# A two-layer kernel on one core: 512 instead of 288 columns a matmul in the second product, the last 64 columns of two blocks as a pair of column tiles

## Chip, cores, metric

The kernel runs on one core of one Trainium2 chip. The metric is the device time of one execution in microseconds; lower is better. The granted TensorE clock is the share of its full speed that the profiler recorded.

## The reference

```python
B, S, D, F = 1, 2048, 576, 4608          # all bf16
def reference(x, w1, b1, w2, b2):
    h = einsum("bsd,df->bsf", x, w1) + b1      # first product, 576 -> 4608
    r = where(h > 0, h, 0)
    h = r * r
    return einsum("bsf,fd->bsd", h, w2) + b2   # second product, 4608 -> 576
```

The output has 576 columns, which is 512 + 64. The widest matmul of these kernels writes 512 columns of float32, which fills one of the program's tiles in PSUM, the memory that matmuls write to.

## The kernel before

The 2048 rows go through in four blocks of 512 (`SB`). For each block the first product makes the hidden tile `hT`, transposed: 36 pieces of 128 hidden columns by 512 rows. The second product takes 128 rows of it at a time as weights (a "row block", 16 in all) and streams `w2` past them, 576 output columns in two halves of 288 (`DH`), 36 steps each.

```python
    DH = D // 2                                   # 288
    # ... weights and x are loaded; x is transposed into xT ...

    def a_rows(sb, ...):                          # most of the first product: pairs of 64-row tiles
        for j in range(NJ):
            # ...
            for i in range(NC):
                keep(nc.tensor.matmul(bx[:], lhsT=w1_h[0:H, LO_C[i], jc], rhs=xT[0:H, LO_W[i], :], ...))
                keep(nc.tensor.matmul(by[:], lhsT=w1_h[H:P, UP_C[i], jc], rhs=xT[H:P, UP_W[i], :], ...))
            evac_h(...)                           # ScalarE: relu + bias; VectorE: square, into hT

    def a_full(sb, order):                        # four pieces: full-array matmuls of 512 columns
        # ... and two pairs of 64-row tiles, `pair`; then evac_h

    def phase_b(sb, hT, last=False, dups=()):     # second product
        for jj in range(RT):                      # 4 row blocks
            # ...
            po = [ps_o.tile([P, 512], FP32, name="po", tag="po") for _ in range(2)]
            o_sb = opool.tile([P, D], BF16, name="o_sb", tag="o_sb")

            def mmb(i, ft, h):
                keep(nc.tensor.matmul(
                    po[h][:, 0:DH],
                    lhsT=hT[:, ft, jj * P:(jj + 1) * P],
                    rhs=w2_sb[:, ft, h * DH:(h + 1) * DH],
                    start=(i == 0), stop=(i == NFT - 1)))

            def evac(h):                          # VectorE: + b2, to bf16
                keep(nc.vector.tensor_tensor(out=o_sb[:, h * DH:(h + 1) * DH], in0=po[h][:, 0:DH],
                                             in1=b2_bc[:, h * DH:(h + 1) * DH], op=ALU.add))

            if last and jj == RT - 1:             # very last row block: one half after the other
                for h in range(2):
                    for i, ft in enumerate(ft_order):
                        mmb(i, ft, h)
                    evac(h)
                    keep(nc.sync.dma_start(out=out2[...], in_=o_sb[:, h * DH:(h + 1) * DH]))
                continue
            for i, ft in enumerate(ft_order):
                for h in range(2):
                    mmb(i, ft, h)
            for h in range(2):
                evac(h)
            keep(nc.sync.dma_start(out=out2[rt * P:(rt + 1) * P, :], in_=o_sb[:]))

    # order of the stages
    a_full(0, "k_outer"); a_rows(0, ...); a_rows(1); a_full(1, "rows_first")
    phase_b(0, ...); phase_b(1, ...)
    a_full(2, "g_outer"); a_rows(2); a_rows(3); a_full(3, "rows_first")
    phase_b(2, ...); phase_b(3, ..., last=True)
```

Of the kernel before, what the change touches and what calls it, by code (L numbers as in the profile page):

```python
# [9 lines left out]
ACT = mybir.ActivationFunctionType  # L10
ALU = mybir.AluOpType
BF16 = mybir.dt.bfloat16
FP32 = mybir.dt.float32
# [4 lines left out]
def kernel(  # L18
# [9 lines left out]
    nc = tc.nc  # L28
    keep = tc.keep_in_program_order
    P = 128  # L30
    H = 64
    x2 = x.flatten_outer_dims()
    out2 = out.flatten_outer_dims()
    S, D = x2.shape
    F = w1.shape[1]
    NFT = F // P
    NC = D // H
    NK = NC // 2
    G = 4
# [3 lines left out]
    assert D == 576 and S % 512 == 0 and F % (2 * P) == 0  # L43
    SB = 512
    RT = SB // P
    DH = D // 2

    const = ctx.enter_context(tc.tile_pool(name="const", bufs=1))
    wpool = ctx.enter_context(tc.tile_pool(name="wpool", bufs=1))
# [1 line left out]
    hpool = ctx.enter_context(tc.tile_pool(name="hpool", bufs=2))  # L51
    rpool = ctx.enter_context(tc.tile_pool(name="rpool", bufs=4))
    opool = ctx.enter_context(tc.tile_pool(name="opool", bufs=3))
    ps_h = ctx.enter_context(tc.tile_pool(name="ps_h", bufs=4, space=PSUM))
    ps_o = ctx.enter_context(tc.tile_pool(name="ps_o", bufs=4, space=PSUM))

# [18 lines left out]
    def load_w1n8(eng, h):  # L75
        src = w1[NK * P:D, 0:GW].rearrange("p (i h f) -> p i h f", h=2, f=P)
        keep(eng.dma_start(out=w1n8[h * H:(h + 1) * H, :, :], in_=src[:, :, h, :]))
# [16 lines left out]
    nc.gpsimd.dma_start(out=b1_rows[0:NFT, :], in_=b1.rearrange("(ft p) -> ft p", p=P))  # L94
    load_w1n8(nc.gpsimd, 0)
    load_w1n8(nc.gpsimd, 1)
    warm = const.tile([P, 1], FP32, name="warm")
    keep(nc.scalar.activation(out=warm[:], in_=nc.const_aps.tensor(0.0, [P, 1], FP32), func=ACT.Relu))  # L98

# [11 lines left out]
    def dup_windows(sb):  # L111
        xT = xT_blk[sb]
        keep(nc.vector.tensor_copy(out=xT[0:H, SPC:SPC + 4, :], in_=xT[H:P, E3:E3 + 4, :]))  # L113
        keep(nc.vector.tensor_copy(out=xT[H:P, SPC:SPC + 4, :], in_=xT[0:H, O:O + 4, :]))  # L114
# [8 lines left out]
    w2_sb = wpool.tile([P, NFT, D], BF16, name="w2_sb")  # L123
# [6 lines left out]
    b2_bc = const.tile([P, D], BF16, name="b2_bc")  # L130
# [18 lines left out]
    def make_b1T():  # L149
        b1T_ps = ps_o.tile([P, P], BF16, name="b1T_ps", tag="po")  # L150
        keep(nc.tensor.transpose(b1T_ps[:], b1_rows[:], ident[:]))  # L151
        keep(nc.vector.tensor_copy(out=b1T[:], in_=b1T_ps[:, 0:NFT]))

    hTs = {}
# [4 lines left out]
    def evac_h(sb, bank, ft):  # L159
        r = rpool.tile([P, SB], BF16, name="r", tag="r")  # L160
        keep(nc.scalar.activation(out=r[:], in_=bank[:], func=ACT.Relu, bias=b1T[:, ft:ft + 1], scale=1.0))  # L161
        keep(nc.vector.tensor_tensor(out=hTs[sb][:, ft, :], in0=r[:], in1=r[:], op=ALU.mult))  # L162

    def a_rows(sb, dup_at=None, dup_sb=None):
        xT = xT_blk[sb]
        for j in range(NJ):
            if j == dup_at:
                dup_windows(dup_sb)
            bx = ps_h.tile([P, SB], FP32, name="ph", tag="ph")
            by = ps_h.tile([P, SB], FP32, name="ph", tag="ph")  # L170
            jc = slice(j * P, (j + 1) * P)
            for i in range(NC):
                keep(nc.tensor.matmul(bx[:], lhsT=w1_h[0:H, LO_C[i], jc], rhs=xT[0:H, LO_W[i], :],  # L173
                                 start=(i == 0), stop=(i == NC - 1)))
                keep(nc.tensor.matmul(by[:], lhsT=w1_h[H:P, UP_C[i], jc], rhs=xT[H:P, UP_W[i], :],  # L175
                                 start=(i == 0), stop=(i == NC - 1)))
            evac_h(sb, bx, G + j)
            evac_h(sb, by, G + NJ + j)

    def a_full(sb, order):  # L180
        xT = xT_blk[sb]
        banks = []
        for g in range(G):
            pool, tag = (ps_o, "po") if g < 2 else (ps_h, "ph")
            banks.append(pool.tile([P, SB], FP32, name="pn", tag=tag))

        def pair(i, start, stop):
            keep(nc.tensor.matmul(banks[2 * i][:], lhsT=w1n8[0:H, i, :], rhs=xT[0:H, SPC, :],  # L188
                             start=start, stop=stop))
            keep(nc.tensor.matmul(banks[2 * i + 1][:], lhsT=w1n8[H:P, i, :], rhs=xT[H:P, E3, :],  # L190
                             start=start, stop=stop))

        def full(g, k, start, stop):
            keep(nc.tensor.matmul(banks[g][:], lhsT=w1n[:, k, g * P:(g + 1) * P], rhs=xT[:, O + k, :],  # L194
                             start=start, stop=stop))

        if order == "rows_first":
            for i in (1, 0):
                pair(i, True, False)
            for g in (2, 3, 0, 1):  # L200
                for k in range(NK):
                    full(g, k, False, k == NK - 1)
                evac_h(sb, banks[g], g)
        else:
            if order == "k_outer":
                for k in range(NK):
                    for g in range(G):
                        full(g, k, k == 0, False)
                    if k == 1:
                        make_b1T()  # L210
            else:
                for g in (2, 3, 0, 1):
                    for k in range(NK):
                        full(g, k, k == 0, False)
            for i in (1, 0):
                pair(i, False, True)
                evac_h(sb, banks[2 * i], 2 * i)
                evac_h(sb, banks[2 * i + 1], 2 * i + 1)

    ft_order = list(range(G))  # L220
    for j in range(NJ):
        ft_order += [G + j, G + NJ + j]

    def phase_b(sb, hT, last=False, dups=()):
        for jj in range(RT):
            if jj < len(dups):
                dup_windows(dups[jj])
            rt = sb * RT + jj
            po = [ps_o.tile([P, 512], FP32, name="po", tag="po") for _ in range(2)]
            o_sb = opool.tile([P, D], BF16, name="o_sb", tag="o_sb")  # L230

            def mmb(i, ft, h):
                keep(nc.tensor.matmul(  # L233
                    po[h][:, 0:DH],
                    lhsT=hT[:, ft, jj * P:(jj + 1) * P],
                    rhs=w2_sb[:, ft, h * DH:(h + 1) * DH],
                    start=(i == 0),
                    stop=(i == NFT - 1),
                ))

            def evac(h):
                keep(nc.vector.tensor_tensor(  # L242
                    out=o_sb[:, h * DH:(h + 1) * DH],
                    in0=po[h][:, 0:DH],
                    in1=b2_bc[:, h * DH:(h + 1) * DH],
                    op=ALU.add,
                ))

            if last and jj == RT - 1:
                for h in range(2):  # L250
                    for i, ft in enumerate(ft_order):
                        mmb(i, ft, h)
                    evac(h)
                    keep(nc.sync.dma_start(out=out2[rt * P:(rt + 1) * P, h * DH:(h + 1) * DH], in_=o_sb[:, h * DH:(h + 1) * DH]))
                continue
            for i, ft in enumerate(ft_order):
                for h in range(2):
                    mmb(i, ft, h)
            for h in range(2):
                evac(h)  # L260
            keep(nc.sync.dma_start(out=out2[rt * P:(rt + 1) * P, :], in_=o_sb[:]))

    for (j0, j1) in [(0, 1), (1, 2), (2, 4), (4, 6), (6, 8), (8, 10), (10, 12)]:
        load_w1(nc.sync, 0, j0, j1)
# [14 lines left out]
    load_xT(3)  # L279
    a_rows(1)  # L280
    a_full(1, "rows_first")
    phase_b(0, hTs[0], dups=(2, 3))
    phase_b(1, hTs[1])
    alloc_hT(2)
    a_full(2, "g_outer")
    a_rows(2)
    alloc_hT(3)
    a_rows(3)
    a_full(3, "rows_first")
    phase_b(2, hTs[2])  # L290
    phase_b(3, hTs[3], last=True)

# [29 lines left out]
```

## Time and profile before

| | before |
|---|---|
| time, median of the first 3 runs | 292.98 us (292.62 to 293.26) |
| profiled execution: time, span | 292.11 us, 290.3 us |
| PE busy | 285.7 us, 98% |
| second product | 1152 matmuls of 288 columns, 141.4 us busy, in two stretches |

These lines are from the page of the kernel before (PE is TensorE's matmuls, PEld its weight loads, DVE VectorE, ACT ScalarE, POOL GpSimd; L233 is line 233 of the kernel): the busy time of each engine, the shares of the chain of waits (the chain that ended last, by engine and by line), and groups of instructions. In a group the columns are busy time, mean ns of one, and idle time of the engine before them. A group's busy time counts overlapping instructions once, so busy time divided by count is the pace, while the mean of one is its length from start to end.

```profile
PE 285.7 (98%) x2409; PEld 178.0 (61%) x2412; DVE 81.5 (28%) x189; ACT 94.2 (32%) x154; POOL 2.7 (1%) x10
...
PE 98%; ACT 0%; issue 0%; DVE 0%
PE po L233 49%; PE ph L173 42%; PE pn L194 5%; PE wps L61 1%; PE ph L175 1%; PE pn L188 1%; PE ta L138 0%; ACT xTw L143 0%; DVE o_sb L242 0%; ACT xTw L144 0%; PE tb L141 0%; PE tb L142 0%; PE b1T_ps L151 0%; PE pn L190 0%
...
L233 PE MATMUL po<-w_sb,hT 128*128 128x288 bf16 x1152 | 141.4, 286 | 0.0
L233 PEld LDWEIGHTS <-hT 128*128 128x128 bf16 x1152 | 112.7, 98 | 28.8
...
L194 PE MATMUL pn<-xTw,w1n 128*128 128x512 bf16 x61 | 14.0, 379 | 0.8 <-ACT xTw L143 0.4
L194 PEld LDWEIGHTS <-w1n 128*128 128x128 bf16 x64 | 6.0, 98 | 8.0 <-issue 1.4
...
L242 DVE TENSOR_TENSOR o_sb<-po,b_bc 128x288 bf16<-128x288 f32 x32 | 13.3, 453 | 123.9 <-PE po L233 123.9
```

PE is busy for 98% of the span, and 98% of the chain is PE: no other engine is what the end waits for, apart from the start, the last addition and its store. The 1152 matmuls of line 233 took 141.4 us, 122.7 ns apiece, though each lasts 286 ns: they are pipelined. Their weight loads last 98 ns each and hide behind them.

The chain in order of time (start, length, what) shows the two stretches of the second product and the last addition.

```profile
72.67 3.40 PE pn L194 x15
76.07 70.56 PE po L233 x576
...
216.77 70.58 PE po L233 x576
287.37 0.46 DVE o_sb L242
```

A stretch of 576 matmuls takes 70.56 us, which is 122.5 ns each. This is the timeline where row tiles (64 x 128) give way to full-array matmuls (128 x 128):

```profile
71.91 0.38 PE L188 MATMUL pn<-xTw,w1n_89 64*128 64x512 bf16 x1
71.92 0.38 PE L190 MATMUL pn<-xTw,w1n_89 64*128 64x512 bf16 x1
72.13 0.38 PE L188 MATMUL pn<-xTw,w1n_89 64*128 64x512 bf16 x1
72.13 0.38 PE L190 MATMUL pn<-xTw,w1n_89 64*128 64x512 bf16 x1
72.67 0.59 PE L194 MATMUL pn<-xTw,w1n 128*128 128x512 bf16 x2 [0.16 <-issue]
```

Row tiles come in pairs, 0.01 us apart or less, and a pair follows the last after 0.22 us. The first full matmul starts 0.54 us after the last pair.

### The profile page before, as it was taken

The numbers are of one execution on the slowest core, as the hardware profiler recorded it, in microseconds if no ns is written. First come the engines' busy times: TensorE is split into PE (matmuls) and PEld (weight loads), VectorE is DVE, ScalarE is ACT, GpSimd is POOL, SyncE is SP. The second block draws the span as 40 slices with busy tenths as digits, with TensorE's granted clock in tenths as the row PEclk, the third lists the DMA queues.
The fourth block names the chain that finished last, engine by engine and source line by source line (L and its number), as shares of the span: only waits on it lengthen the run. The fifth ranks groups of instructions, "written<-read, shape, count | busy, mean of one in ns | idle before, by whom it ended". The sixth has DMA issues, their size and how long they took to land.

```text
span 290.3 us, 5455 instructions
## 1 busy us (share of the span) xinstructions
PE 285.7 (98%) x2409; PEld 178.0 (61%) x2412; DVE 81.5 (28%) x189; ACT 94.2 (32%) x154; POOL 2.7 (1%) x10
## 2 busy tenths in 40 slices
PE   8999999999999999999999999999999999999995
PEld 4444444444677777777744444444447777777774
DVE  3344544444531011110025444444440111100111
ACT  4566666666400000000027666666670000000000
POOL 3000000000000000000000000000000000000000
PEclk9999999999999999999999999999999999999999
DMA  7999999900000000000000000000000000000000
GB/s 203 214 212 177 255 357 265 164 1 2 0 23 0 23 20 20 23 3 20 20 23 0 3 0 2 0 2 0 2 0 2 20 24 20 21 2 23 20 20 24
DMA packets 27096, 16.05 MB, mean 55 GB/s; under 512 B 11028, under 2 KB 27040, under 8 KB 27072
## 3 DMA queue, kind: packets, MB, share of 16 engines
q1 hardware_dynamic: 26688, 15.32, 23.9%
q8 instruction: 19, 0.31, 0.4%
q10 hardware_dynamic: 288, 0.30, 0.3%
q0 software_dynamic: 96, 0.07, 0.1%
q14 instruction: 5, 0.04, 0.0%
HBM read 11.36 MB, written 2.36 MB: 47 GB/s over the span
## 4 chain that ended last, share of the span: by engine, by line
PE 98%; ACT 0%; issue 0%; DVE 0%
PE po L233 49%; PE ph L173 42%; PE pn L194 5%; PE wps L61 1%; PE ph L175 1%; PE pn L188 1%; PE ta L138 0%; ACT xTw L143 0%; DVE o_sb L242 0%; ACT xTw L144 0%; PE tb L141 0%; PE tb L142 0%; PE b1T_ps L151 0%; PE pn L190 0%
## 5 line engine op out<-in xcount | busy, mean ns | idle before, releaser
L233 PE MATMUL po<-w_sb,hT 128*128 128x288 bf16 x1152 | 141.4, 286 | 0.0
L233 PEld LDWEIGHTS <-hT 128*128 128x128 bf16 x1152 | 112.7, 98 | 28.8
L173 PE MATMUL ph<-xTw,w_h 64*128 64x512 bf16 x576 | 124.6, 376 | 0.0
L175 PE MATMUL ph<-xTw,w_h 64*128 64x512 bf16 x576 | 124.6, 376 | 0.0
L173 PEld LDWEIGHTS <-w_h 64*128 64x128 bf16 x576 | 54.1, 94 | 68.3
L161 ACT ACTIVATE r<-ph,b1T 128x512 bf16<-128x512 f32 x128 | 81.1, 685 | 41.6 <-PE ph L175 41.6
L162 DVE TENSOR_TENSOR hT<-r 128x512 bf16<-128x512 bf16 x144 | 61.2, 426 | 77.3 <-ACT r L161 76.7
L175 PEld LDWEIGHTS <-w_h 64*128 64x128 bf16 x576 | 54.1, 94 | 0.0
L242 DVE TENSOR_TENSOR o_sb<-po,b_bc 128x288 bf16<-128x288 f32 x32 | 13.3, 453 | 123.9 <-PE po L233 123.9
L161 ACT ACTIVATE r<-pn,b1T 128x512 bf16<-128x512 f32 x16 | 10.3, 688 | 78.8 <-PE pn L190 77.5
L194 PE MATMUL pn<-xTw,w1n 128*128 128x512 bf16 x61 | 14.0, 379 | 0.8 <-ACT xTw L143 0.4
L194 PEld LDWEIGHTS <-w1n 128*128 128x128 bf16 x64 | 6.0, 98 | 8.0 <-issue 1.4
L61 PE MATMUL wps<-const-bfloat16-1.0 128*128 128x512 bf16 (+1 forms) x7 | 2.9, 594 | 0.8 <-PEq L306 0.8
L113 DVE COPY xTw<-xTw 64x2048 bf16<-64x2048 bf16 x4 | 2.8, 690 | 0.4 <-ACT xTw L144 0.3
L114 DVE COPY xTw<-xTw 64x2048 bf16<-64x2048 bf16 x4 | 2.7, 687 | 0.1
L139 DVE COPY xTw<-ta 128x384 bf16<-128x384 bf16 x4 | 1.3, 358 | 4.2 <-PE ta L138 4.2
L188 PE MATMUL pn<-xTw,w1n_89 64*128 64x512 bf16 x8 | 2.4, 379 | 0.0
L190 PE MATMUL pn<-xTw,w1n_89 64*128 64x512 bf16 x8 | 2.4, 379 | 0.0
L61 PEld LDWEIGHTS <-const-bfloat16-1.0 128*128 128x128 bf16 x7 | 0.9, 135 | 2.1 <-issue 2.1
L98 ACT ACT_TABLE_LOAD x1 | 1.3, 1283 | 1.7 <-PEq L306 1.7
L138 PE MATMUL ta<-ident,x_sb 128*128 128x128 bf16 x12 | 1.6, 265 | 0.0
L143 ACT COPY xTw<-tb 128x128 bf16<-128x128 bf16 x4 | 1.1, 282 | 1.2 <-PE tb L142 1.1
(21 smaller groups left out, 10.2 us busy)
## 6 DMA issues: line engine op xcount, KB each, us to landing
w_sb<-in_w_dram SPq DMA_DIRECT2D x6, 864.0 KB, 11.4
w_h<-in_w_dram SPq DMA_DIRECT2D x14, 288.0 KB, 7.4
out_dram<-o_sb SPq DMA_DIRECT2D x15, 144.0 KB, 1.8
w_h<-in_w_dram SPq DMA_DIRECT2D x4, 144.0 KB, 4.1
w1n<-in_w_dram SPq DMA_DIRECT2D x4, 128.0 KB, 4.0
x_sb<-in_x_dram ACTq DMA_DIRECT2D x2, 144.0 KB, 3.0
x_sb<-in_x_dram SPq DMA_DIRECT2D x2, 144.0 KB, 2.8
b_bc<-in_b_dram SPq DMA_DIRECT2D x1, 144.0 KB, 7.6
```

The costliest lines, as they stand in the source:

```text
L61: keep(nc.tensor.matmul(wps[:, 0:n], lhsT=ones[:, 0:P], rhs=ones[:, 0:n], start=True, stop=True))
L113: keep(nc.vector.tensor_copy(out=xT[0:H, SPC:SPC + 4, :], in_=xT[H:P, E3:E3 + 4, :]))
L114: keep(nc.vector.tensor_copy(out=xT[H:P, SPC:SPC + 4, :], in_=xT[0:H, O:O + 4, :]))
L161: keep(nc.scalar.activation(out=r[:], in_=bank[:], func=ACT.Relu, bias=b1T[:, ft:ft + 1], scale=1.0))
L162: keep(nc.vector.tensor_tensor(out=hTs[sb][:, ft, :], in0=r[:], in1=r[:], op=ALU.mult))
L173: keep(nc.tensor.matmul(bx[:], lhsT=w1_h[0:H, LO_C[i], jc], rhs=xT[0:H, LO_W[i], :], start=(i == 0), stop=(i == NC - 1)))
L175: keep(nc.tensor.matmul(by[:], lhsT=w1_h[H:P, UP_C[i], jc], rhs=xT[H:P, UP_W[i], :], start=(i == 0), stop=(i == NC - 1)))
L188: keep(nc.tensor.matmul(banks[2 * i][:], lhsT=w1n8[0:H, i, :], rhs=xT[0:H, SPC, :], start=start, stop=stop))
L190: keep(nc.tensor.matmul(banks[2 * i + 1][:], lhsT=w1n8[H:P, i, :], rhs=xT[H:P, E3, :], start=start, stop=stop))
L194: keep(nc.tensor.matmul(banks[g][:], lhsT=w1n[:, k, g * P:(g + 1) * P], rhs=xT[:, O + k, :], start=start, stop=stop))
L233: keep(nc.tensor.matmul(po[h][:, 0:DH], lhsT=hT[:, ft, jj * P:(jj + 1) * P], rhs=w2_sb[:, ft, h * DH:(h + 1) * DH], start=(i == 0), stop=( ...
L242: keep(nc.vector.tensor_tensor(out=o_sb[:, h * DH:(h + 1) * DH], in0=po[h][:, 0:DH], in1=b2_bc[:, h * DH:(h + 1) * DH], op=ALU.add,))
```

## The change

The intent is fewer instructions for the same columns. Each row block now streams 512 columns in one matmul instead of 2 x 288. The last 64 columns are computed with the roles exchanged: the 64 columns of `w2` are the weights, and the hidden tile, 512 rows of it, streams past. Weights of 64 columns fill half of the array's columns, so two blocks are put side by side as column tiles (128 x 64), writing to partitions 0 to 63 and 64 to 127 of one PSUM tile (`phase_t`, once for each pair of blocks). The result is transposed, so a DMA turns it before it is stored. The very last row block is cut in pieces of 224, 160 and 128 columns, so that the last addition and store are small. The diff, shortened:

```diff
-    DH = D // 2
+    DM = 512
+    DT = D - DM
@@
+    b2_col = const.tile([P, 1], BF16, name="b2_col")
+    for h in range(2):
+        nc.gpsimd.dma_start(out=b2_col[h * DT:(h + 1) * DT, :], in_=b2[DM:D].rearrange("(d o) -> d o", o=1))
+    b2T = const.tile([P, 1], FP32, name="b2T")
+    nc.gpsimd.tensor_copy(out=b2T[:], in_=b2_col[:])
@@
+    t_order = ft_order[G:] + ft_order[:G]
+    EDGES = [0, 224, 384, 512]
+
+    def phase_t(sb):
+        pt = ps_o.tile([P, SB], FP32, name="pt", tag="po")
+        for i, ft in enumerate(t_order):
+            for h in range(2):
+                keep(nc.tensor.matmul(pt[h * DT:(h + 1) * DT, :], lhsT=w2_sb[:, ft, DM:D], rhs=hTs[sb + h][:, ft, :],
+                                      start=(i == 0), stop=(i == NFT - 1)))
+        oT = tpool.tile([P, SB], BF16, name="oT", tag="oT")
+        keep(nc.scalar.activation(out=oT[:], in_=pt[:], func=ACT.Identity, bias=b2T[:], scale=1.0))
+        ot = tpool.tile([P, RT, P], BF16, name="ot", tag="ot")
+        keep(nc.sync.dma_start_transpose(out=ot[:, :, :], in_=oT[:, :]))
+        for h in range(2):
+            r0 = (sb + h) * SB
+            dst = out2[r0:r0 + SB, DM:D].rearrange("(j p) d -> p j d", p=P)
+            keep(nc.sync.dma_start(out=dst, in_=ot[:, :, h * DT:(h + 1) * DT]))
@@ phase_b: the two halves, their additions and the staged last block are removed (cut here); in their place
+            o_sb = opool.tile([P, DM], BF16, name="o_sb", tag="o_sb")
+            edges = EDGES if last and jj == RT - 1 else [0, DM]
+            for d0, d1 in zip(edges, edges[1:]):
+                po = ps_o.tile([P, 512], FP32, name="po", tag="po")
+                for i, ft in enumerate(ft_order):
+                    keep(nc.tensor.matmul(po[:, 0:d1 - d0], lhsT=hT[:, ft, jj * P:(jj + 1) * P],
+                                          rhs=w2_sb[:, ft, d0:d1], start=(i == 0), stop=(i == NFT - 1)))
+                keep(nc.vector.tensor_tensor(out=o_sb[:, d0:d1], in0=po[:, 0:d1 - d0], in1=b2_bc[:, d0:d1], op=ALU.add))
+                keep(nc.sync.dma_start(out=out2[rt * P:(rt + 1) * P, d0:d1], in_=o_sb[:, d0:d1]))
@@ order of the stages
     a_full(1, "rows_first")
+    phase_t(0)
     phase_b(0, hTs[0], dups=(2, 3))
@@
     a_full(3, "rows_first")
+    phase_t(2)
     phase_b(2, hTs[2])
```

More of the change, by code (lines that the diff above doesn't have):

```diff
@@ L53 @@
     opool = ctx.enter_context(tc.tile_pool(name="opool", bufs=3))
+    tpool = ctx.enter_context(tc.tile_pool(name="tpool", bufs=2))
     ps_h = ctx.enter_context(tc.tile_pool(name="ps_h", bufs=4, space=PSUM))
@@ L228, in phase_b @@
             rt = sb * RT + jj
-            po = [ps_o.tile([P, 512], FP32, name="po", tag="po") for _ in range(2)]
-            o_sb = opool.tile([P, D], BF16, name="o_sb", tag="o_sb")
-            def mmb(i, ft, h):
-                keep(nc.tensor.matmul(
-                    po[h][:, 0:DH],
-                    lhsT=hT[:, ft, jj * P:(jj + 1) * P],
-                    rhs=w2_sb[:, ft, h * DH:(h + 1) * DH],
-                    start=(i == 0),
-                    stop=(i == NFT - 1),
-                ))
-            def evac(h):
-                keep(nc.vector.tensor_tensor(
-                    out=o_sb[:, h * DH:(h + 1) * DH],
-                    in0=po[h][:, 0:DH],
-                    in1=b2_bc[:, h * DH:(h + 1) * DH],
-                    op=ALU.add,
-                ))
-            if last and jj == RT - 1:
-                for h in range(2):
-                    for i, ft in enumerate(ft_order):
-                        mmb(i, ft, h)
-                    evac(h)
-                    keep(nc.sync.dma_start(out=out2[rt * P:(rt + 1) * P, h * DH:(h + 1) * DH], in_=o_sb[:, h * DH:(h + 1) * DH]))
-                continue
-            for i, ft in enumerate(ft_order):
-                for h in range(2):
-                    mmb(i, ft, h)
-            for h in range(2):
-                evac(h)
-            keep(nc.sync.dma_start(out=out2[rt * P:(rt + 1) * P, :], in_=o_sb[:]))
+            o_sb = opool.tile([P, DM], BF16, name="o_sb", tag="o_sb")
[7 more added lines that the diff above has]
+                keep(nc.sync.dma_start(out=out2[rt * P:(rt + 1) * P, d0:d1], in_=o_sb[:, d0:d1]))
     for (j0, j1) in [(0, 1), (1, 2), (2, 4), (4, 6), (6, 8), (8, 10), (10, 12)]:
```

## The prediction

> **What bounds it now.** TensorE. The page gives PE 98% busy, the chain of waits is 98% PE, and in the list of waits matmuls waited 1.5 us in all, before 6 us. The granted clock is 1.000. So only TensorE's stream, or the tail behind it, can count. The second product is 49% of the chain: two stretches of 70.56 us, 576 matmuls of 288 columns each, 122.5 ns a matmul.
>
> **Fixed cost of a matmul.** The Trainium skill, "TensorE: Matmul & The Clock Gate", Part 1, states N/2.4 + about 2.5 ns. This trace agrees: 122.5 ns for 288 columns; 512-column full matmuls start about every 216 ns, and so do pairs of 64-row tiles, whose two start within 10 ns.
>
> **What the change does on TensorE.** Columns streamed do not fall, if column tiles run two at a time: per row block 2 x 288 = 512 + 64, and the 64 return as 72 pairs of 512 columns. Only instruction overhead goes.
> - Removed: 1152 x 122.5 ns = 141.1 us.
> - Added: 16 row blocks x 36 x 215.8 ns = 124.3 us, and 72 pairs x 215.8 ns = 15.5 us. Net -1.3 us.
> - The last block is cut in 224, 160 and 128 columns: 72 more instructions, +0.2 us. A weight load lasts 98 ns, longer than a 128-column matmul streams, but loads overlap: the warm 128-column transposes near 4.8 us start 55 ns apart, each with its own load. I expect no load limit.
> - Four new changes of tiling. The skill, "TensorEngine Tiling (Array Packing)", Key Properties, says that a mode change drains the engine; here full to row tiles (149.70 to 150.01 us) costs 0.1 us extra, row tiles to full (72.13 to 72.67 us) 0.3 us. Estimate +0.8 us.
> - Tail: the last addition is 128 instead of 288 columns (0.46 us now) and its store smaller: about -0.3 us.
>
> Sum about -0.6 us, all on the critical path.
>
> **Off the path.** Additions of 512 columns (estimate 0.7 us) against 7.8 us of matmuls per block; one activation of about 0.7 us per pair of blocks on an idle ScalarE; the transposing DMA (those of x land in 5.6 us) and stores of 128-byte rows, behind 60 us of matmuls. The new stage reads the second block's hidden tile just after its last pieces are computed, but takes those four last, some 7 us later, while their evacuation ends 1.1 us after the matmuls; waits go by region in this trace (matmuls at 5.71 us read a tile that VectorE is still filling). I expect no new wait of TensorE.
>
> **Predicted time.** 292.4 us; 80% range 290.8 to 296.0. Faster by over 2%: 0.01; within 2%: 0.84; slower by over 2%: 0.15.
>
> **What would show it.** Pairs of the new stage start together, every 216 ns; the stage takes 15.5 us, twice; row blocks 7.77 us each; small gaps at the stage's ends; PE still 98%; the last block about 8 us.
>
> **What would make it wrong.** Mainly column tiles that do not overlap. No trace here shows a column tile; row tiles feed each half of the rows once, column tiles stream two operands through all 128. One after the other, the stage doubles: +15.5 us, about 308 us, 5% slower. The tiling page also says that column tiling disables fast weight load: if the 64-column loads show, each 25 ns in a pair costs 1.8 us. If 128-column pieces were limited by loads at 98 ns, the last block would cost 2.5 us more. A wait of TensorE at the new stage's start would cost about 1 us each.

One sentence of it is worded wrongly: "the stage takes 15.5 us, twice". The 72 pairs of its own sum are those of both stages together, so 15.5 us is the total and each stage was due at 7.8 us. The predicted time uses the total.

## More of the kernel before

One line carries a warning: line 194 has 61 matmuls and 64 weight loads. The program issues one load for each matmul, so three matmul records are missing from this trace.

## The result

The changed kernel took 291.44 us (median of 4 runs, 291.28 to 291.98) against 292.80 us (4 runs). The ratio was 0.9954, 95% interval 0.9936 to 0.9973. A ratio is the mean time of one kernel's fast runs over that of the other's of the same rounds, so it is not quite the ratio of the medians. With five rounds of unchanged copies (told below) the ratio was 0.9975, interval 0.9957 to 0.9992. The change is a gain, and a small one: well within 2%.

The page of the changed kernel, the same parts:

```profile
PE 285.7 (99%) x2052; PEld 134.1 (46%) x2052; DVE 79.7 (28%) x175; ACT 95.7 (33%) x156; POOL 4.2 (1%) x13
...
PE 98%; ACT 0%; DVE 0%; issue 0%
PE po L259 43%; PE ph L180 42%; PE pt L238 5%; PE pn L201 5%; PE wps L63 1%; PE ph L182 1%; PE pn L195 1%; PE ta L145 0%; ACT xTw L150 0%; ACT xTw L151 0%; DVE o_sb L261 0%; PE tb L149 0%; PE tb L148 0%; PE b1T_ps L158 0%; PE pn L197 0%
...
L259 PE MATMUL po<-w_sb,hT 128*128 128x512 bf16 (+3 forms) x648 | 124.8, 355 | 0.0
...
L259 PEld LDWEIGHTS <-hT 128*128 128x128 bf16 x648 | 60.7, 98 | 64.3 <-issue 0.8
...
L261 DVE TENSOR_TENSOR o_sb<-po,b_bc 128x512 bf16<-128x512 f32 (+3 forms) x18 | 11.4, 633 | 125.0 <-PE po L259 125.0
...
L238 PE MATMUL pt<-hT,w_sb 128*64 128x512 bf16 x144 | 15.9, 380 | 0.0
...
L238 PEld LDWEIGHTS <-w_sb 128*64 128x64 bf16 x144 | 8.0, 110 | 7.8 <-issue 0.8
...
L201 PE MATMUL pn<-xTw,w1n 128*128 128x512 bf16 x64 | 14.5, 379 | 0.4 <-ACT xTw L150 0.4
```

PE still fills the span. Line 238 is the new stage: 144 matmuls, each 380 ns long, in 15.9 us. That is 110 ns apiece for 512 columns, which is only possible two at a time. Its weight loads became longer (110 ns, against 94 for a row tile's and 98 for a full one), and they hide too. The busy time of weight loads in the second product fell from 112.7 to 68.7 us (60.7 + 8.0), and the kernel did not become faster by anything like that: these loads were hidden behind matmuls before and after.

The chain in order of time, and the groups of line 259 with the widths kept apart:

```profile
72.75 3.56 PE pn L201 x16
76.31 7.89 PE pt L238 x72
84.21 62.27 PE po L259 x288
...
216.62 7.89 PE pt L238 x72
224.50 62.46 PE po L259 x360
286.99 0.29 DVE o_sb L261
```

```profile
L259 PE MATMUL po<-w_sb,hT 128*128 128x512 bf16 x540 | 116.9, 379 | 0.0
...
L259 PE MATMUL po<-w_sb,hT 128*128 128x224 bf16 x36 | 3.6, 259 | 0.0
...
L259 PE MATMUL po<-w_sb,hT 128*128 128x160 bf16 x36 | 2.7, 233 | 0.0
...
L259 PE MATMUL po<-w_sb,hT 128*128 128x128 bf16 x36 | 2.2, 219 | 0.0
```

For each pair of blocks there is now one piece of 7.89 us (column tiles) and one of 62.3 to 62.5 us, in place of one of 70.56. There is no gap in which PE waited for the hidden tile, which the new stage reads right after it is made. What there is at the change of tiling is small. These two lines of the timeline show the last full matmul and the start of the new stage (two pairs):

```profile
75.94 0.38 PE L201 MATMUL pn<-xTw,w1n 128*128 128x512 bf16 x1
76.25 0.62 PE L238 MATMUL pt<-hT,w_sb 128*64 128x512 bf16 x4
```

They start 0.31 us apart, where two full matmuls of 512 columns start 0.216 us apart.

To compare traces exactly I use the start of every matmul record. These times are worked out from the records of the packed trace; no view of the profile prints them. I call "stream" the time from the first row-tile matmul of `a_rows` (line 173, in the changed kernel 180) to the end of the last matmul, and "tail" what follows to the end of the span. The start, before the stream, is the same code in both kernels but for two tiny loads and a copy of their result, and it varied between 9.64 and 10.43 us over the profiles, in both kinds of kernel alike.

| us | before | its copy | after | its copy |
|---|---|---|---|---|
| start | 9.75 | 10.09 | 10.00 | 9.99 |
| stream | 277.579 | 277.578 | 276.951 | 276.951 |
| tail | 3.01 | 3.01 | 2.79 | 2.78 |

The stream of a copy repeats within 1 ns. With the change it became 0.63 us shorter, and the tail 0.22 us. So the trace accounts for 0.85 us of gain, and the spans differ by 0.6 us only because the profiled run of before happened to start 0.25 us earlier.

### The profile page after: what moved, and what is told of

It is laid out like the page before. It is cut to its first block, busy times and chain, and to the rows that moved or that the text cites. A ratio compares the mean times of both kernels' runs of the same rounds, so it can differ in the third digit from the quotient of the medians.

```text
span 289.7 us, 4742 instructions
## 1 busy us (share of the span) xinstructions
PE 285.7 (99%) x2052; PEld 134.1 (46%) x2052; DVE 79.7 (28%) x175; ACT 95.7 (33%) x156; POOL 4.2 (1%) x13
## 4 chain that ended last, share of the span: by engine, by line
PE 98%; ACT 0%; DVE 0%; issue 0%
PE po L259 43%; PE ph L180 42%; PE pt L238 5%; PE pn L201 5%; PE wps L63 1%; PE ph L182 1%; PE pn L195 1%; PE ta L145 0%; ACT xTw L150 0%; ACT xTw L151 0%; DVE o_sb L261 0%; PE tb L149 0%; PE tb L148 0%; PE b1T_ps L158 0%; PE pn L197 0%
## 5 line engine op out<-in xcount | busy, mean ns | idle before, releaser
L259 PE MATMUL po<-w_sb,hT 128*128 128x512 bf16 (+3 forms) x648 | 124.8, 355 | 0.0
L259 PEld LDWEIGHTS <-hT 128*128 128x128 bf16 x648 | 60.7, 98 | 64.3 <-issue 0.8
L261 DVE TENSOR_TENSOR o_sb<-po,b_bc 128x512 bf16<-128x512 f32 (+3 forms) x18 | 11.4, 633 | 125.0 <-PE po L259 125.0
L238 PE MATMUL pt<-hT,w_sb 128*64 128x512 bf16 x144 | 15.9, 380 | 0.0
L238 PEld LDWEIGHTS <-w_sb 128*64 128x64 bf16 x144 | 8.0, 110 | 7.8 <-issue 0.8
L241 ACT ACTIVATE oT<-pt,b2T 128x512 bf16<-128x512 f32 x2 | 1.4, 687 | 14.5 <-PE pt L238 14.5
```

The lines of the kernel that those rows point to most:

```text
L238: keep(nc.tensor.matmul(pt[h * DT:(h + 1) * DT, :], lhsT=w2_sb[:, ft, DM:D], rhs=hTs[sb + h][:, ft, :], start=(i == 0), stop=(i == NFT - 1)))
L259: keep(nc.tensor.matmul(po[:, 0:d1 - d0], lhsT=hT[:, ft, jj * P:(jj + 1) * P], rhs=w2_sb[:, ft, d0:d1], start=(i == 0), stop=(i == NFT - 1)))
L261: keep(nc.vector.tensor_tensor(out=o_sb[:, d0:d1], in0=po[:, 0:d1 - d0], in1=b2_bc[:, d0:d1], op=ALU.add))
```

## The experiments

My theory: TensorE pays about 2.5 ns for each matmul on top of its columns, the change saves some of those and pays for changes of tiling, and everything else is hidden. The rivals: the gain is that of fewer weight loads, or that of a shorter tail, and the column tiles might not really overlap. In the diffs below, `-` is the changed kernel, unless before is named.

### Unchanged copies of both kernels

> An unchanged copy of the kernel before, as a control: how much do start, stream and tail vary from run to run? Expected ratio to before 1.000 within 0.002. Its profile gives a second reading of the start (first matmul of the first product at 5.71 us in before, 5.96 us in after) and of the stream from there to the last matmul (281.6 us in before).

> An unchanged copy of the changed kernel. The two traces account for only 0.6 us of gain (stream 0.63 us shorter between the first product's row tiles and the last matmul, tail 0.22 us shorter, start 0.25 us later), while the timed runs gave 0.9954, that is 1.35 us. If the trace accounts for all, with the late start as accident: ratio 0.997 (-0.85 us). If there is a further gain that the profiled pair hid: 0.9954 again, and the start no later than in the control.

Measured: the copy of before has ratio 1.001 (0.9994 to 1.0025), 292.70 us; the copy of the changed kernel 0.9975 (0.9957 to 0.9992), 291.78 against 292.58 us. By the ratio that is a gain of 0.73 us, close to the 0.85 us of the trace. The 1.35 us of the first measurement was not repeated. Its interval and this one overlap, and no trace shows a further saving. What the excess was is left open; the varying start, up to 0.8 us, is large enough to be it, but this was not shown.

The copy of before corrects a reading as well. Here is the same change of tiling in its timeline:

```profile
72.47 0.38 PE L188 MATMUL pn<-xTw,w1n 64*128 64x512 bf16 x1
72.47 0.38 PE L190 MATMUL pn<-xTw,w1n 64*128 64x512 bf16 x1
72.78 0.39 PE L194 MATMUL pn<-xTw,w1n 128*128 128x512 bf16 x1
```

The first full matmul starts 0.31 us after the last pair, not 0.54. This trace has all 64 matmuls of line 194, 16 of them in this stage. The first trace has 15 here (the `x15` of the chain line at 72.67 us), and the difference in the gap, 0.23 us, is about the length of one slot: the first matmul of the stage had no record, and I had read the hole as a cost of the hardware.

### The number of matmuls doubled

```diff
 (against before, shortened)
-            for i, ft in enumerate(ft_order):
-                for h in range(2):
-                    mmb(i, ft, h)                       # 2 x 288 columns
+            for q in range(4):                          # 4 x 144 columns, a tile each
+                po = ps_o.tile([P, 512], FP32, name="po", tag="po")
+                for i, ft in enumerate(ft_order):
+                    keep(nc.tensor.matmul(po[:, 0:DQ], lhsT=hT[:, ft, jj * P:(jj + 1) * P],
+                                          rhs=w2_sb[:, ft, d0:d1], start=(i == 0), stop=(i == NFT - 1)))
+                ...                                     # addition of 144 columns
```

> The kernel before with each row block in four pieces of 144 columns, each with its own bank, in place of two of 288: same columns, 1152 more matmuls and weight loads. Theory (a fixed cost of about 2.5 ns a matmul, weight loads hidden): one matmul every 62.5 ns, stream +2.9 us, last addition 0.15 us shorter: about +2.7 us, ratio 1.009. Rival 1 (only columns count, the gain is elsewhere): within 0.3 us of before. Rival 2 (the weight load of 98 ns cannot be pipelined): one matmul every 98 ns, +41 us.

Measured: 295.06 us, ratio 1.0096 (1.0077 to 1.0114). The stream grew by 2.88 us, from 277.578 to 280.458, for 1152 matmuls more: 2.50 ns each. From its chain in order of time:

```profile
76.28 72.00 PE po L235 x1152
...
218.42 72.01 PE po L235 x1152
290.46 0.31 DVE o_sb L237
```

A stretch of 1152 matmuls takes 72.00 us, so 62.5 ns for 144 columns. The rate can be had from the widths alone: 512 columns take 215.9 ns (62.17 us for 288 matmuls in the changed kernel), 288 take 122.5, so a column costs (215.9 - 122.5) / 224 = 0.417 ns, and 2.5 ns are left over at any width. The fixed cost is real, and it is what the change saves in the stream.

### The weight loads doubled, matmuls unchanged

```diff
 (against before)
             def mmb(i, ft, h):
+                keep(nc.tensor.ldweights(hT[:, ft, jj * P:(jj + 1) * P]))
                 keep(nc.tensor.matmul(
```

> The kernel before with one extra weight load, of the same weights, ahead of each matmul of the second product: 1152 more loads, no more matmuls. Theory (the fixed cost belongs to the matmul, loads are hidden as long as they fit): two loads in 122.5 ns at about 55 ns each fit: within 0.5 us of before. Rival (the cost that the change removes is that of weight loads): at least the 2.5 ns for each, +2.9 us; if extra loads cannot be hidden at all, 55 ns each, +63 us.

Measured: 292.25 us, ratio 0.9988 (0.9971 to 1.0005). The stream is 277.578 us, the same to the nanosecond. From its groups of instructions, shapes kept apart:

```profile
L234 PE MATMUL po<-w_sb,hT 128*128 128x288 bf16 x1152 | 141.4, 286 | 0.0
...
L233 PEld LDWEIGHTS <-hT 128*128 128x128 bf16 x1152 | 112.7, 98 | 0.4
L234 PEld LDWEIGHTS <-hT 128*128 128x128 bf16 x1152 | 110.2, 96 | 0.0
```

Two loads, 96 and 98 ns long, fit into each slot of 122.5 ns; they start 42 and 81 ns apart in turn, so they overlap each other. Weight loads are not what the change saved, although their busy time is what fell most on its page.

### The column tiles made to follow each other

```diff
-        pt = ps_o.tile([P, SB], FP32, name="pt", tag="po")
+        pts = [ps_o.tile([P, SB], FP32, name="pt", tag="po") for _ in range(2)]
-                keep(nc.tensor.matmul(pt[h * DT:(h + 1) * DT, :], lhsT=w2_sb[:, ft, DM:D], ...
+                keep(nc.tensor.matmul(pts[h][0:DT, :], lhsT=w2_sb[:, ft, DM:D], ...
```

The activation is done in two halves, so that the result stays right.

> The changed kernel with both blocks of the 64-column stage written to the same column tile (output rows 0 to 63 of two banks), so that the two matmuls of a step cannot run side by side; same matmuls, weights, columns. Theory (column tiles run two at a time, and that pays for the 64 columns): the stage takes 144 x 215.8 ns / 2 = 15.5 us instead of 7.9, twice: +15.4 us, about 307 us. Rival (the two were never really parallel, the stage is short for another reason): no change.

Measured: 307.30 us, ratio 1.0502 (1.0487 to 1.0518). The stream grew by 15.53 us, and each stage from 7.89 to 15.66 us. From its groups of instructions, shapes kept apart:

```profile
L238 PE MATMUL pt<-hT,w_sb 128*64 128x512 bf16 x144 | 31.5, 379 | 0.0
L238 PEld LDWEIGHTS <-w_sb 128*64 128x64 bf16 x144 | 15.7, 110 | 15.7 <-issue 0.8
```

The same 144 matmuls with the same length of 379 ns now take 31.5 us. In the changed kernel the two of a pair start 3 to 4 ns apart, and their loads, too, run side by side (8.0 us there, 15.7 here). Side-by-side column tiles are what makes the change possible; without them it would have cost 5%.

### No column tiles: 512 and 64 columns as two plain matmuls

```diff
+            for i, ft in enumerate(ft_order):
+                for h, (d0, d1) in enumerate([(0, DM), (DM, D)]):      # 512, then 64, same weights
+                    keep(nc.tensor.matmul(po[h][:, 0:d1 - d0], lhsT=hT[:, ft, jj * P:(jj + 1) * P],
+                                          rhs=w2_sb[:, ft, d0:d1], start=(i == 0), stop=(i == NFT - 1)))
 (phase_t, its pool, its loads and its calls removed; D columns stored at once, last block not cut)
```

> 512 columns an instruction without the column tiles: the last 64 columns as a second matmul of 64 columns with the same hidden tile as weights, per row block, as plain full-array matmuls. Number of matmuls as before (1152). Theory (cost of a matmul = columns/2.4 + 2.5 ns, but no faster than weight loads can follow each other, of which I know only that 55 ns works): if a load every 29 ns is possible, the sum is that of before, 292.8 us; if 55 ns is their limit, each 64-column matmul takes 55 instead of 29 ns: +15 us, 308 us. If a load takes its full 98 ns: +40 us, 333 us.

Measured: 293.95 us, ratio 1.0039 (1.0016 to 1.0063). The stream is 277.578 us, exactly that of before: 1152 matmuls then and now, and the sum does not care that they are 512 and 64 wide. A load limit of 55 ns is excluded. The 1.05 us by which its tail is longer (4.06 us) is my own doing: I left out the staged last block, so 0.9 us of addition (0.69 + 0.21) and the whole store come after the last matmul.

```profile
L240 DVE TENSOR_TENSOR o_sb<-po,b_bc 128x512 bf16<-128x512 f32 x16 | 11.1, 692 | 124.4 <-PE po L237 124.4
...
L240 DVE TENSOR_TENSOR o_sb<-po,b_bc 128x64 bf16<-128x64 f32 x16 | 3.4, 214 | 0.0
```

So wide matmuls alone gain nothing. What gains is that 64-column matmuls, 576 of them, are replaced by 72 pairs.

### More changes of tiling

```diff
-    def phase_t(sb):
-        pt = ps_o.tile(...)
-        for i, ft in enumerate(t_order):
+    CUTS = [0, 5, 10, 15, 20, 24, 28, 32, 36]
+    def part_t(sb, n):                                  # one part ahead of each of the 8 row blocks
+        if n == 0:
+            pts[sb] = ps_h.tile([P, SB], FP32, name="pt", tag="ph")
+        pt = pts[sb]
+        for i in range(CUTS[n], CUTS[n + 1]):
+            ft = t_order[i]
             ...
+        if n < 7:
+            return
```

> The changed kernel with the column-tile stage cut into eight parts, one ahead of each row block: 32 changes of tiling in place of 4 at this place, all else equal. Reading of the changed kernel's trace: 309 to 312 ns from the last matmul of one mode to the first of the next, against 216 within a mode, so about 95 ns a change: 28 x 95 ns = +2.7 us. The prediction's estimate (0.1 us into tiles, 0.3 us out of them, the latter read across what looks like a missing record) would give 28 x 0.2 = +5.6 us. If a change cost nothing: 0.

Measured: 294.47 us, ratio 1.0066 (1.0048 to 1.0084). The stream grew by 3.18 us, 0.114 us for each of the 28 changes. From its chain in order of time:

```profile
85.40 1.20 PE pt L244 x10
86.60 6.15 PE po L268 x28
```

A part of five pairs takes 1.20 us. Five pairs at 0.216 us are 1.08, so 0.12 us goes at its ends here, and another 0.1 us into the last matmul ahead of it, which is 309 ns from the next start instead of 216. The cost is near my corrected reading (+2.7) and far from the prediction's (+5.6). My reading counted only the gap at the change itself (309 to 312 ns instead of 216). In the records the next slot is longer too: the second pair of a part starts 236 or 237 ns after the first, and the second matmul after a part mostly 226 or 227 ns after the first. For 14 parts more that adds about 0.4 us.

### The last row block in one piece

```diff
-    EDGES = [0, 224, 384, 512]
+    EDGES = [0, 512]
```

> The changed kernel with the last row block as one piece of 512 columns, not 224, 160 and 128. Theory (the gain is mostly instruction count, the tail little): stream 0.18 us shorter, last addition 0.40 us longer (692 against 293 ns), last store about 0.2 us longer: +0.4 us against the changed kernel, ratio to before still about 0.997. Rival (the gain comes from the shorter tail): most of the gain is lost, ratio to before 0.999 to 1.000.

Measured: 292.00 us, ratio 0.9985 (0.9967 to 1.0004), between the theory and the rival, and the interval holds both. The trace is finer: stream 0.18 us shorter (276.770), as expected, tail 0.75 us longer (3.54), so 0.57 us worse in all. I had underrated the tail. Of the 0.85 us that the change gains, only 0.28 are left without the cut. But the tail does not explain the gain: before had a staged last block of its own, and its tail was only 0.22 us longer.

### Other cuts of the last row block

```diff
-    EDGES = [0, 224, 384, 512]
+    EDGES = [0, 448, 512]        # and, as a kernel of its own, [0, 384, 512]
```

> The changed kernel with the last row block in two pieces, 448 and 64 columns, in place of 224, 160 and 128. 36 matmuls of 64 columns then follow each other with nothing wider between them to hide their loads of 128 x 128 behind. If loads can follow each other every 29 ns: stream 36 x 2.5 = 0.09 us shorter, last addition some 0.07 us shorter: -0.15 us against the changed kernel. If 55 ns is their limit (the shortest distance seen between such loads one after another): stream +0.85 us. If 98 ns: +2.4 us.

> The changed kernel with the last row block in two pieces, 384 and 128 columns: one set of 36 matmuls less, the last piece as in the changed kernel. The fixed cost read from the traces says stream 0.09 us shorter, tail the same: -0.09 us, to be seen in the trace and not in the times. It would be the fastest of the kernels here, if only by that.

Measured: with 448 and 64 columns 291.93 us, ratio 0.9974 (0.9961 to 0.9988), with 384 and 128 columns 291.53 us, ratio 0.9966 (0.9953 to 0.9979). Neither can be told from the changed kernel by time. In the traces both streams are 0.09 us shorter (276.861 and 276.860), as the fixed cost says. With 64 columns the tail is 0.07 us shorter too (2.72), so the whole is 0.16 us better, as expected. With 128 the tail was 0.47 us longer in the one profile, mostly because its last store landed 1.88 us after its issue instead of 1.47; whether that belongs to this cut or to the run is open.

From the groups of the kernel with 448 and 64 columns, shapes kept apart:

```profile
L259 PE MATMUL po<-w_sb,hT 128*128 128x448 bf16 x36 | 7.0, 352 | 0.0
...
L259 PE MATMUL po<-w_sb,hT 128*128 128x64 bf16 x36 | 1.2, 193 | 0.0
```

36 matmuls of 64 columns take 1.2 us: 35 steps of 29 ns and one length of 193 ns. Each has a 128 x 128 weight load of its own, and nothing wider stands between them. So loads that last 98 ns can follow each other every 29 ns.

### The second column-tile stage at the very end

```diff
-    phase_t(2)
     phase_b(2, hTs[2])
-    phase_b(3, hTs[3], last=True)
+    phase_b(3, hTs[3])
+    phase_t(2)
```

> The changed kernel with the second column-tile stage moved behind all row blocks, to the end, where nothing hides its activation, transposing DMA and stores. Theory (they cost 0.69 + 2.3 + 1.9 us and lie off the critical path in the changed kernel): stream about as before, and the tail grows from 2.8 us by about 3 us: +3 us against the changed kernel, 294.7 us. Rival (they delay something already, through the queue of the stores): less than 1 us more.

Measured: 295.04 us, ratio 1.0083 (1.0069 to 1.0097). The tail grew from 2.79 to 6.52 us, and the stream is 0.29 us shorter (no cut, one change of tiling less). From its timeline near the end:

```profile
286.87 0.69 ACT L241 ACTIVATE oT<-pt,b2T 128x512 bf16<-128x512 f32 x1 [69.37 <-PE pt L238]
287.58 1.20 SPq L243 DMA_TRANSPOSE ot<-oT  x1
289.93 0.93 SPq L247 DMA_DIRECT2D out_dram<-ot  x2
```

So the theory holds (about +3 us expected; against the copy of the changed kernel the ratio is 0.0108 higher, which is 3.2 us, and the trace is 3.4 us longer from the start of the stream), and the rival, less than 1 us, is out. After the last matmul come the activation, the issue of the transposing DMA, which lands 2.3 us later, and then the two stores. In the changed kernel the same chain starts at 84.3 and at 224.5 us, under 62 us of matmuls, and no wait of TensorE comes of it.

## Why the prediction was right

The predicted 292.4 us and its range (290.8 to 296.0) hold the measured 291.44. The mechanism was the predicted one. The number alone says less: the range is 5.2 us wide, and the measured gain of 1.36 us is more than double the predicted 0.6. The centre was missed by 0.9 us: 0.2 because the kernel before took 292.80 us over the four runs of the comparison and not the 292.98 that I started from, 0.25 by the terms below, and 0.5 by the excess of the first measurement, which stays open. What supports the prediction is that its terms were found in the traces, not that the number lies in its range. The terms, in us:

| term | predicted | traces |
|---|---|---|
| 1152 matmuls of 288 -> 576 of 512 and 72 pairs | -1.3 | -1.24 |
| last block in three pieces | +0.2 | +0.18 |
| four changes of tiling | +0.8 | +0.43 |
| tail | -0.3 | -0.22 |
| sum | -0.6 | -0.85 |

- The first term is 141.12 - (576 + 72) x 0.21587, with 0.21587 us (62.17 / 288) both for a 512-column matmul and for a pair. The fixed cost behind it was shown by doubling the matmuls (+2.50 ns each), and its rival, the weight loads, was ruled out by doubling the loads (0.00 us).
- The second term is the stream of the uncut kernel against that of the changed one.
- The third term is what is left of the stream's 0.63 us, and it agrees with 4 x 0.114 us = 0.45 us from the kernel with 32 changes. The starts in the changed kernel's own trace give it directly: 309 ns into a stage and 311 to 312 out of it instead of 216, and 237 and 226 ns for the slot after each change, 0.22 us a stage and 0.44 in all. It is the one that was mis-sized: "row tiles to full (72.13 to 72.67 us) 0.3 us". The trace lacked a matmul record there; with it, the start is 0.31 us after the last pair, so 0.1 us extra. The hint was on the page: 61 matmuls against 64 weight loads.
- The fourth term was sized rightly against before, but its importance was hidden by the small difference: the cut is worth 0.57 us against no cut.
- "I expect no load limit" was right, and more so than I knew: the limit that I had evidence for was 55 ns, and 29 ns works.
- The main risk, column tiles that do not overlap, did not come true; had it come true, the time would have been near that of the serial kernel, 307.3 us and 5% slower (I had said about 308). The loads of 64 columns did last longer, 110 ns, but nothing showed; that they do because fast weight load is off was not shown.
- "I expect no new wait of TensorE" was right: PE stays at 98% of the chain, and the transposing DMA is hidden, as moving it to the end showed.

## What to carry to other kernels

When PE fills the chain, add up columns first: if a rewrite streams the same columns, what it can save in the stream is the fixed cost of the matmuls that it removes, here 2.5 ns each, 1.24 us of 293 for the 504 slots saved (1152 down to 576 and 72 pairs), and changes of tiling take some of that back, here 0.43 us. What follows the last matmul is counted apart: cutting the last row block was worth 0.57 us. The busy time of what is hidden, such as weight loads, can halve without moving the time. And before a gap in a trace is read as a cost of the hardware, count the records: a matmul without a record leaves a gap just like a stall.

## What the Trainium skill lacked or had wrong

- "TensorE: Matmul & The Clock Gate", Part 2, "Back-to-back issue gap", gives for sustained pairs of load and matmul about 81 ns at N=128 and about 131 ns at N=512, and says that its isolated formula, N/2.4 + 2.5 ns, is off there. Here such pairs run at 55.8 and 215.9 ns, and the isolated formula fits every width that was run: 29 ns for 64 columns, 62.5 for 144, 122.5 for 288.
- The same page, Part 3, "What overlaps and what doesn't", says that weight loads overlap matmuls in flight only when the row group differs, though Part 2 of the page also allows it for a load into the background weight buffer. Here full-array loads hide completely: two loads of 96 and 98 ns in every slot of 122.5 ns, with no change of the stream.
- The same page, Part 2, "LDWEIGHTS", has a load last P/1.2 for P columns, which comes to an estimated 53 ns for 64 columns and 107 for 128. Here a load of 64 columns for a column tile lasts 110 ns and one of 128 columns for the whole array 98 ns, and the latter can follow each other every 29 ns.
- "TensorEngine Tiling (Array Packing)", Key Properties, says that a change of mode drains the engine and gives no figure. Here one costs about 0.11 us.
- No page has a measured time for two 64-column tiles side by side. Here a pair of 512 columns takes 0.216 us, the same as a pair of 64-row tiles.
